# Windowed attention into a sine MLP: casting loads, denominators staged a unit ahead, Q copies on another engine, chunk tiles for x, one-bank MLP tiles

## The chip, the cores and the metric

The kernel runs on one core of one Trainium2 chip. The metric is the device time of one execution in microseconds (us), median of several; lower is better. A profile covers a slightly shorter span, from the first to the last instruction: 572.6 us for an execution that took 574.28 by the clock outside.

Engines are named as in the profile: PE is TensorE (PEld is its weight load), DVE is VectorE, ACT is ScalarE, POOL is GpSimd, SP is SyncE. In this kernel an instruction that is late also holds up what stands behind it on its engine: POOL's copies for batch 0, whose input DVE had ready at 82.9 us, ran only at 99.41, behind weight casts and load issues.

## The reference, cut to what matters

```python
# q, k, v: (8 batches, 8 heads, 576 tokens, 64);  8 global tokens
scores = (q @ k.T) / 8
mask   = (|i - j| <= 32) | is_global[i] | is_global[j]
attn   = softmax(where(mask, scores, -1e9)) @ v
x      = attn as (4608 tokens, 512)
h      = x @ w_in                      # 512 -> 2048
g      = h + sin(alpha * h)**2 / alpha
out    = g @ w_out                     # 2048 -> 512
```

## The kernel before

For each batch the kernel does attention in eight *units* (four pairs of heads, two halves of the token windows). The MLP works on nine chunks of 512 tokens. A steady *period* is: the first half of the MLP for one chunk ("MLP-in"), a short attention prologue, eight units of the next batch interleaved with the second half of the MLP ("MLP-out"), and an end that writes the eight global queries' columns. A unit, with cuts marked:

```python
def stage_V(b, hp, par, E, xTb, gn, gd):
    num = psA.tile([P, 2, CH], F32, name="num")      # one PSUM buffer of each name
    den = psA.tile([P, NU, QC], F32, name="den")
    ... # PE: den <- E by ones (2 matmuls); num <- E by V (6 matmuls)
    nc.scalar.activation(out=lnd[:], in_=den[:], func=AF.Ln)
    nc.scalar.activation(out=rec[:], in_=lnd[:], func=AF.Exp, scale=-1.0)   # 1/den
    for t in range(2):
        nc.vector.tensor_tensor(out=xTb..., in0=num..., in1=rec..., op=ALU.mult)  # products
    for t in range(2):
        nc.vector.tensor_reduce(out=gn..., in_=num[global columns], ...)
    nc.vector.tensor_reduce(out=gd..., in_=den[global columns], ...)        # last reader of den
```

MLP-in uses tiles of one or two PSUM banks in turn, and alpha has been folded into the weights on chip:

```python
CYC = (("h2", 1), ("num", 2), ("den", 1), ("Sp", 2))      # PSUM tiles, banks
h2 = w_inp @ x            # w_inp = w_in * alpha, cast to bf16 on DVE / POOL
Sb = sin(h2)              # ACT, up to two banks at once
S2 = Sb * Sb              # POOL, and DVE for a second bank
H2b = h2 + S2             # DVE;   w_outp = w_out / alpha on POOL
```

The Q transposes of the next batch sit inside MLP-in, and DVE copied them from PSUM (`qBD <- h2`). The eight global columns are written by POOL (`xTb[:, :, index] = xg`), and DVE then copies the batch into one tile for all of x.

The softmax here doesn't subtract the row's maximum and nothing guards it: scores larger than these inputs give would overflow.

Of the kernel before, what the change touches and what calls it, by code (L numbers as in the profile page):

```python
# [12 lines left out]
ALU = mybir.AluOpType  # L13
# [5 lines left out]
def kernel(  # L19
# [28 lines left out]
    NU = S // (2 * QB)  # L48
# [12 lines left out]
    rpool = ctx.enter_context(tc.tile_pool(name="rpool", bufs=2))  # L61
    xbp = ctx.enter_context(tc.tile_pool(name="xbp", bufs=2))
    gpool = ctx.enter_context(tc.tile_pool(name="gpool", bufs=2))

    psA = ctx.enter_context(
        tc.tile_pool(name="psA", bufs=1, space=bass.MemoryType.PSUM)
    )
# [5 lines left out]
    MASK = const.tile([P, 2, NU, QC], BF, name="MASK")  # L73
    w_inp = const.tile([P, CT, DFF], BF, name="w_inp")
    w_outp = const.tile([P, NT, DM], BF, name="w_outp")
    xT = const.tile([P, CT, NTOK], BF, name="xT")
    kTw = [const.tile([P, 2, NU, P], BF, name=f"kTw{i}") for i in range(NHP)]
    qBD = [const.tile([P, 2, NU, 2, QC], BF, name=f"qBD{i}") for i in range(NHP)]
# [3 lines left out]
    Kps = psA.tile([P, 2 * CH], BF, name="Kps")  # L82

    for i in range(2):
        nc.vector.memset(VW[i][0:32, 0, 0, :], 0.0)
        nc.vector.memset(VW[i][64:128, 1, NU - 1, :], 0.0)
        nc.vector.memset(VW[i][96:128, :, :, :], 0.0)


    def load_slots(b, split):  # L90
# [4 lines left out]
        slots = []  # L95
# [19 lines left out]
        for i in range(H if split else NTW):  # L115
            for src, dst in ((k, KS), (q, QS)):
                slots.append(partial(by_head if split else by_tile, src, dst, i))
# [19 lines left out]
    qk = {}  # L137
    for f in load_slots(0, True):
        f()


    make_identity(nc, identb[:])
    nc.vector.memset(ones0[:], 0.0)
# [6 lines left out]
    nc.vector.memset(Kps[:].bitcast(F32), 0.0)  # L150

    setup = tc.alloc_tile_pool(name="setup", bufs=1)
    gidx = setup.tile([1, NG], DT.int64, name="gidx")
    nc.sync.dma_start(out=gidx[:], in_=global_idx[None, :])
    gsc = const.tile([1, 2 * NG], DT.int32, name="gsc")
    nc.sync.dma_start(out=gsc[:].bitcast(DT.int64), in_=global_idx[None, :])

    gall = setup.tile([P, NG], DT.int64, name="gall")
    nc.sync.dma_start(
# [5 lines left out]
    nc.sync.dma_start(out=gcol[KB : KB + NG, :], in_=global_idx[:, None])  # L165
    gN = [setup.tile([NG * B, DM], F32, name=f"gN{i}") for i in range(3)]
    regs = {}

    def gather(i, src, eng, js):
        for j in js:  # L170
            if (eng, j) not in regs:
                regs[eng, j] = eng.value_load(
                    gsc[0:1, 2 * j : 2 * j + 1], min_val=0, max_val=S - 1
                )
            eng.dma_start(  # L175
                out=gN[i][j : NG * B : NG, :].rearrange("b (h d) -> b h d", d=D),
                in_=src[:, :, bass.ds(regs[eng, j], 1), :].rearrange("b h o d -> b h (o d)"),
            )

    gather(0, k, nc.sync, range(NG))  # L180
    gather(1, q, nc.scalar, range(NG))
    gather(2, v, nc.sync, range(0, NG, 2))
    gather(2, v, nc.scalar, range(1, NG, 2))
# [5 lines left out]
    nc.vector.tensor_copy(out=Gp[:], in_=gcol[:].bitcast(DT.int32)[:, 0:1])  # L189

# [14 lines left out]
    nc.gpsimd.affine_select(  # L205
        out=flag[:], in_=flag[:], compare_op=ALU.is_ge, fill=0.0,
        base=-KB, channel_multiplier=1, pattern=[[0, 1]],
    )
    nc.gpsimd.affine_select(
        out=flag[:], in_=flag[:], compare_op=ALU.is_ge, fill=0.0,  # L210
        base=KB + NG - 1, channel_multiplier=-1, pattern=[[0, 1]],
    )

    MB = setup.tile([P, NU, 2, QC], F32, name="MB")
    nc.gpsimd.memset(MB[:], 1.0)
    bandp = [[0, NU], [0, 2], [1, QB]]
    MBq = MB[:, :, :, 0:QB]

    nc.gpsimd.affine_select(
        out=MBq, in_=MBq, compare_op=ALU.is_ge, fill=0.0,  # L220
        base=0, channel_multiplier=1, pattern=[[0, NU], [0, 2], [-1, QB]],
    )

    nc.gpsimd.affine_select(
        out=MBq, in_=MBq, compare_op=ALU.is_ge, fill=0.0,
        base=2 * WIN, channel_multiplier=-1, pattern=bandp,
    )

    nc.gpsimd.affine_select(
        out=MBq, in_=MBq, compare_op=ALU.is_ge, fill=0.0,  # L230
        base=-WIN, channel_multiplier=1, pattern=[[2 * QB, NU], [QB, 2], [0, QB]],
    )
    nc.gpsimd.affine_select(
        out=MBq, in_=MBq, compare_op=ALU.is_ge, fill=0.0,
        base=S - 1 + WIN, channel_multiplier=-1, pattern=[[-2 * QB, NU], [-QB, 2], [0, QB]],
    )

    nc.gpsimd.affine_select(
        out=MBq, in_=MBq, compare_op=ALU.is_ge, fill=0.0,
        base=KB - 1, channel_multiplier=-1, pattern=[[0, NU], [0, 2], [0, QB]],  # L240
    )

    MBg = MB[:, :, :, QB:QC]
    nc.gpsimd.affine_select(
        out=MBg, in_=MBg, compare_op=ALU.is_ge, fill=0.0,
        base=-WIN, channel_multiplier=1, pattern=[[0, NU], [0, 2], [0, NG]],
    )
    nc.gpsimd.affine_select(
        out=MBg, in_=MBg, compare_op=ALU.is_ge, fill=0.0,
        base=WIN + QB - 1, channel_multiplier=-1, pattern=[[0, NU], [0, 2], [0, NG]],  # L250
    )
# [13 lines left out]
        out=MBq, in0=MBq, in1=DQ[:].rearrange("p (u a c) -> p u a c", a=2, c=QB),  # L265
        op=ALU.max,
    )
    nc.vector.tensor_copy(out=MASK[:].rearrange("p a u c -> p u a c"), in_=MB[:])

# [4 lines left out]
    nc.vector.tensor_copy(out=VgN[:], in_=gN[2][:])  # L274
    gps = psA.tile([P, 2, NHP, NG * B], BF, name="ops")
# [9 lines left out]
    )  # L285
    setup.release()
    pregs = [
# [3 lines left out]


    def globals_in(b, hp):
        nc.gpsimd.tensor_copy(
            out=kTw[hp][:, :, :, KB : KB + NG].rearrange("p a u g -> p (a u) g"),
            in_=GT[:, 0, hp, b, None, :].to_broadcast([P, 2 * NU, NG]),
        )
        for t in range(2):
            pr = slice(64 * t, 64 * t + 64)
            nc.gpsimd.tensor_copy(  # L300
                out=qBD[hp][pr, :, :, t, QB:QC].rearrange("p a u g -> p (a u) g"),
                in_=GT[pr, 1, hp, b, None, :].to_broadcast([64, 2 * NU, NG]),
            )

    def stage_T(b, hp):
        QS, KS = qk[b]
        for jt in range(NTW):
# [7 lines left out]
            out=kTw[hp][:, :, :, 0:KB],  # L315
            in_=bass.AP(
                tensor=base.tensor, offset=base.offset,
                ap=[list(base.ap[0]), [QB, 2], [2 * QB, NU], [1, KB]],
            ),
        )  # L320
        Qps = psA.tile([P, S], BF, name="h2")
# [6 lines left out]
        for t in range(2):  # L328
            pr = slice(64 * t, 64 * t + 64)
            nc.vector.tensor_copy(  # L330
                out=qBD[hp][pr, :, :, t, 0:QB].rearrange("p a u c -> p u a c"),
                in_=Qps[pr, :].rearrange("p (u a c) -> p u a c", a=2, c=QB),
            )
# [4 lines left out]
    def stage_Q(b, hp, par):  # L338
        Sp = psA.tile([P, 2, CH], F32, name="Sp")
        for u in range(NU):  # L340
            o = (u % HU) * 2 * QC
            nc.tensor.matmul(  # L342
                out=Sp[:, u // HU, o : o + 2 * QC],
                lhsT=kTw[hp][:, par, u, :],
                rhs=qBD[hp][:, par, u, :, :],
                start=True, stop=True, skip_group_check=True,
            )
# [5 lines left out]
            in1=MASK[:, par, :, None, :].to_broadcast([P, NU, 2, QC]),  # L353
# [4 lines left out]
    def stage_V(b, hp, par, E, xTb, gn, gd):  # L358
        W = VW[b % 2]
        num = psA.tile([P, 2, CH], F32, name="num")  # L360
        den = psA.tile([P, NU, QC], F32, name="den")
        for t, on in enumerate((ones0, ones1)):
# [5 lines left out]
            )  # L368
        for u in range(NU):
            o = (u % HU) * 2 * QC  # L370
            nc.tensor.matmul(
                out=num[:, u // HU, o : o + 2 * QC],
                lhsT=W[:, par, u, hp * P : (hp + 1) * P],
# [3 lines left out]
        lnd = rpool.tile([P, NU, QC], F32, name="lnd")  # L377
        nc.scalar.activation(out=lnd[:], in_=den[:], func=AF.Ln)  # L378
        rec = rpool.tile([P, NU, QC], F32, name="rec")
        nc.scalar.activation(out=rec[:], in_=lnd[:], func=AF.Exp, scale=-1.0)  # L380
        numv = num[:, :, 0:EW].rearrange("p a (u t c) -> p a u t c", t=2, c=QC)
        for t in range(2):
            pr = slice(64 * t, 64 * t + 64)
            xv = xTb[pr, hp, :].rearrange("p (a u r c) -> p a u r c", a=2, u=HU, r=2)
            nc.vector.tensor_tensor(  # L385
                out=xv[:, :, :, par, :],
                in0=numv[pr, :, :, t, 0:QB],
                in1=rec[pr, :, 0:QB].rearrange("p (a u) c -> p a u c", a=2),
                op=ALU.mult,
            )  # L390
        for t in range(2):
            pr = slice(64 * t, 64 * t + 64)
            nc.vector.tensor_reduce(  # L393
                out=gn[pr, par, hp, :],
                in_=numv[pr, :, :, t, QB:QC].rearrange("p a u c -> p c a u"),
                axis=mybir.AxisListType.XY, op=ALU.add,
            )
        nc.vector.tensor_reduce(  # L398
            out=gd[:, par, hp, :],
            in_=den[:, :, QB:QC].rearrange("p u c -> p c u"),  # L400
            axis=mybir.AxisListType.X, op=ALU.add,
# [15 lines left out]

    def attention(b):

        units = [(hp, par) for hp in range(NHP) for par in range(2)]  # L420
        Es = {}
        st = {}

# [241 lines left out]
```

## Time and profile before

575.36 us (573.01 to 576.26, three runs), span 572.6 us. The page of the profile gives each engine's busy time (first fence), and the view of stage windows gives it for one steady period (second fence). Its columns are: the stretch, its length, then for each engine busy us and instruction count, the clock granted to PE (1.00 is full), the DMA share and GB/s. The four rows are MLP-in, prologue, units and end; they sum to 58.2 us.

```profile
PE 362.7 (63%) x2396; PEld 186.8 (33%) x2440; DVE 331.5 (58%) x702; ACT 220.4 (38%) x343; POOL 307.9 (54%) x451
```

```profile
219.00:241.30 22.30, 17.17 (x86) 7.83 (x89) 12.65 (x19) 8.57 (x11) 12.90 (x21) 0.92 0.19 45
241.30:247.20 5.90, 4.13 (x42) 2.40 (x41) 3.97 (x7) 4.47 (x6) 5.32 (x6) 1.00 0.35 24
247.20:274.10 26.90, 18.03 (x152) 10.24 (x154) 18.88 (x56) 12.48 (x24) 11.41 (x16) 1.00 1.10 94
274.10:277.20 3.10, 1.26 (x6) 0.39 (x4) 0.91 (x2) 0.59 (x1) 1.62 (x8) 1.00 0.12 46
```

No engine is full in any stage. What the engines wait for stands in the view of waits (engine, line, result it wanted, what released it, us in total, times, longest):

```profile
PEld L363 <- DVE gd L398: 103.4, 56, 8.0
ACT lnd L378 <- PE den L363: 100.9, 59, 8.4
PE den L363 <- DVE gd L398: 82.4, 56, 7.7
DVE xTb L385 <- ACT rec L380: 57.3, 47, 1.8
PE h_854 L540 <- DVE xT L416: 22.8, 1, 22.8
```

The first four of these waits form a ring (`den` waits for `gd`, `lnd` for `den`, the products for `rec`), which the timeline shows in one unit (start, duration, engine, line, operation; in brackets how long the engine had stood idle and who released it):

```profile
264.00 0.32 PE L363 MATMUL den<-E,ones_77 128*128 128x336 bf16 x1 [1.24 <-DVE gd L398]
264.49 0.45 ACT L378 ACTIVATE lnd<-den 128x336 f32<-128x336 f32 x1 [1.56 <-PE den L363]
264.98 0.48 ACT L380 ACTIVATE rec<-lnd 128x336 f32<-128x336 f32 x1
265.49 0.92 DVE L385 TENSOR_TENSOR xTb<-num,rec 64x288 bf16<-64x288 f32 x2 [1.01 <-ACT rec L380]
266.45 0.42 DVE L393 TENSOR_REDUCE gn<-num 64x8 f32<-64x48 f32 x2
266.88 0.21 DVE L398 TENSOR_REDUCE gd<-den 128x8 f32<-128x48 f32 x1
267.15 0.32 PE L363 MATMUL den<-E,ones_77 128*128 128x336 bf16 x1 [1.54 <-DVE gd L398]
```

There is one `den` buffer. Its last reader is `gd`, a reduction of 0.21 us, which stands behind the products and `gn`; the products need `rec`; `rec` needs `lnd`; `lnd` needs `den`. So a unit takes at least the length of the ring, 3.15 us here.

The start is long too: the first MLP matmul runs at 102.32 us. The groups of instructions show the weight casts on it (count, busy us, mean ns):

```profile
L482 POOL TENSOR_SCALAR w_outp<-wtmp,recipT 128x512 bf16<-128x512 f32 x16 | 25.6, 1609 | 0.1
L466 DVE TENSOR_TENSOR w_inp<-wtmp,alphaB 128x2048 bf16<-128x2048 f32 x2 | 10.6, 5316 | 0.1
```

POOL gets to the eight column copies of batch 0 only at 99.41, behind the `w_outp` casts; DVE's last step before them had ended at 82.9. That is the wait of 22.8 us above.

### The profile page before, as it was taken

The numbers are of one execution on the slowest core, as the hardware profiler recorded it, in microseconds if no ns is written. First come the engines' busy times: TensorE is split into PE (matmuls) and PEld (weight loads), VectorE is DVE, ScalarE is ACT, GpSimd is POOL, SyncE is SP. The second block draws the span as 40 slices with busy tenths as digits, with TensorE's granted clock in tenths as the row PEclk, the third lists the DMA queues.
The fourth block names the chain that finished last, engine by engine and source line by source line (L and its number), as shares of the span: only waits on it lengthen the run. The fifth ranks groups of instructions, "written<-read, shape, count | busy, mean of one in ns | idle before, by whom it ended". The sixth has DMA issues, their size and how long they took to land.

```text
span 572.6 us, 7365 instructions
## 1 busy us (share of the span) xinstructions
PE 362.7 (63%) x2396; PEld 186.8 (33%) x2440; DVE 331.5 (58%) x702; ACT 220.4 (38%) x343; POOL 307.9 (54%) x451
## 2 busy tenths in 40 slices
PE   0124220776586768666866587767676767678996
PEld 0123210334333433243334333433343334333443
DVE  7448940458547854685568536663776476647430
ACT  0013210425444544354435442644364426444431
POOL 9743999459146904690459136832792361037430
PEclk9999999979999999899989988999999989999999
DMA  9977955409630943095309630993099300000011
GB/s 90 113 111 292 279 69 36 64 0 115 53 89 0 125 45 88 1 120 48 89 1 114 54 89 2 81 86 89 0 94 76 88 1 18 20 37 1 37 38 74
DMA packets 132202, 40.48 MB, mean 71 GB/s; under 512 B 123204, under 2 KB 123972, under 8 KB 131524
## 3 DMA queue, kind: packets, MB, share of 16 engines
q0 software_dynamic: 118208, 14.82, 40.8%
q1 hardware_dynamic: 13092, 24.99, 14.1%
q8 instruction: 19, 0.31, 0.2%
q10 hardware_dynamic: 864, 0.20, 0.2%
q14 instruction: 19, 0.16, 0.1%
HBM read 39.47 MB, written 9.44 MB: 85 GB/s over the span
## 4 chain that ended last, share of the span: by engine, by line
issue 28%; POOL 24%; PE 20%; DVE 8%; ACT 7%; DMA 6%; ACTq 3%; SPq 1%; POOLq 0%; DVEq 0%
PE num L540 7%; ACT Sb L547 5%; POOL w_outp L482 4%; PE ops L576 4%; POOL QS L103 3%; POOL KS L103 3%; DVE H2b L525 3%; PE Sp L540 3%; DMA QS<-in_q_dram 2%; POOL VW_92 L110 2%; POOL xTb L413 2%; ACTq L175 2%; DMA wtmp<-in_moe_w_in_dram 2%; POOL w_inp L466 2%; ACT L547 1%
## 5 line engine op out<-in xcount | busy, mean ns | idle before, releaser
L576 PE MATMUL ops<-w_outp,H2b 128*128 128x512 bf16 x412 | 103.1, 379 | 1.7 <-ACT osb L583 0.7
L540 PEld LDWEIGHTS <-w_inp 128*128 128x128 bf16 x576 | 58.3, 104 | 138.2 <-issue 49.8
L385 DVE TENSOR_TENSOR xTb<-num,rec 64x288 bf16<-64x288 f32 x128 | 58.2, 455 | 58.4 <-ACT rec L380 57.3
L413 POOL COPY xTb<-xg 128x4 bf16 x64 | 13.0, 203 | 127.6 <-DVE xg L411 124.1
L363 PE MATMUL den<-E,ones_77 128*128 128x336 bf16 x64 | 21.3, 333 | 89.8 <-DVE gd L398 82.4
L378 ACT ACTIVATE lnd<-den 128x336 f32<-128x336 f32 x64 | 28.9, 452 | 111.8 <-PE den L363 100.9
L576 PEld LDWEIGHTS <-H2b 128*128 128x128 bf16 x576 | 52.2, 98 | 49.0 <-issue 1.0
L349 ACT ACTIVATE E<-Sp 128x672 bf16<-128x672 f32 x64 | 46.6, 729 | 48.0 <-PE Sp L342 47.7
L540 PE MATMUL num<-xT,w_inp 128*128 128x512 bf16 x204 | 58.7, 426 | 4.2 <-DVE H2b L525 3.3
L547 ACT ACTIVATE Sb<-num 128x1024 bf16<-128x1024 f32 x27 | 27.7, 1024 | 37.1 <-PE num L540 34.9
L363 PEld LDWEIGHTS <-ones_77 128*128 128x128 bf16 x64 | 6.2, 97 | 104.2 <-DVE gd L398 103.4
L351 DVE TENSOR_TENSOR E<-E,MASK 128x672 bf16<-128x672 bf16 x64 | 32.6, 512 | 9.3 <-ACT E L349 8.1
L540 PE MATMUL Sp<-xT,w_inp 128*128 128x512 bf16 x140 | 33.6, 379 | 0.2
L103 POOL DMA_DIRECT2D KS<-in_k_dram x42 | 33.0, 786 | 0.0
L103 POOL DMA_DIRECT2D QS<-in_q_dram x42 | 32.4, 772 | 0.0
L380 ACT ACTIVATE rec<-lnd 128x336 f32<-128x336 f32 x64 | 31.0, 484 | 2.0
L547 ACT ACTIVATE Sb<-Sp 128x1024 bf16<-128x1024 f32 x18 | 18.4, 1025 | 30.6 <-PE Sp L540 30.6
L308 PE MATMUL Kps<-identb,KS 96*128 96x96 bf16 x192 | 14.4, 214 | 23.9 <-POOL identb masks.py:199 19.6
L540 PE MATMUL den<-xT,w_inp 128*128 128x512 bf16 x108 | 28.4, 387 | 0.0
L393 DVE TENSOR_REDUCE gn<-num 64x8 f32<-64x48 f32 x128 | 26.2, 205 | 2.6
L583 ACT COPY osb<-ops 128x512 f32<-128x512 f32 x27 | 15.8, 585 | 30.1 <-PE ops L576 30.1
L547 ACT ACT_TABLE_LOAD x8 | 10.3, 1283 | 41.6 <-PE h_854 L540 24.3
(480 smaller groups left out, 758.8 us busy)
## 6 DMA issues: line engine op xcount, KB each, us to landing
out_dram<-osb SPq DMA_DIRECT2D x36, 256.0 KB
wtmp<-in_moe_w_in_dram SPq DMA_DIRECT2D x4, 1024.0 KB
wtmp<-in_moe_w_out_dram SPq DMA_DIRECT2D x4, 1024.0 KB
KS<-in_k_dram POOLq DMA_DIRECT2D x42, 96.0 KB, 4.0
QS<-in_q_dram POOLq DMA_DIRECT2D x42, 96.0 KB, 4.3
VW_91<-in_v_dram POOLq DMA_DIRECT2D x20, 112.0 KB, 4.2
VW_92<-in_v_dram POOLq DMA_DIRECT2D x20, 112.0 KB, 4.2
VW_91<-VW_91 SPq DMA_DIRECT2D x4, 384.0 KB
```

Source lines behind the costliest of these rows:

```text
L103: nc.gpsimd.dma_start(out=dst[:, t, :, :], in_=src[b, :, t * TW : (t + 1) * TW, :].rearrange("h p d -> p h d"),)
L349: nc.scalar.activation(out=E[:], in_=Sp[:, :, 0:EW], func=AF.Exp, scale=scale)
L351: nc.vector.tensor_tensor(out=Ev, in0=Ev, in1=MASK[:, par, :, None, :].to_broadcast([P, NU, 2, QC]), op=ALU.mult,)
L363: nc.tensor.matmul(out=den[:].rearrange("p u c -> p (u c)"), lhsT=on[:], rhs=E[:].rearrange("p a (u t c) -> p (a u) t c", t=2, c=QC)[:, :, ...
L378: nc.scalar.activation(out=lnd[:], in_=den[:], func=AF.Ln)
L380: nc.scalar.activation(out=rec[:], in_=lnd[:], func=AF.Exp, scale=-1.0)
L385: nc.vector.tensor_tensor(out=xv[:, :, :, par, :], in0=numv[pr, :, :, t, 0:QB], in1=rec[pr, :, 0:QB].rearrange("p (a u) c -> p a u c", a=2 ...
L393: nc.vector.tensor_reduce(out=gn[pr, par, hp, :], in_=numv[pr, :, :, t, QB:QC].rearrange("p a u c -> p c a u"), axis=mybir.AxisListType.XY ...
L413: nc.gpsimd.tensor_copy(out=xTb[:, :, bass.ds(pregs[j], 1)], in_=xg[:, :, j : j + 1])
L540: nc.tensor.matmul(out=h2[:, k_, :], lhsT=w_inp[:, ci, (nt + k_) * P : (nt + k_ + 1) * P], rhs=xT[:, ci, t0 : t0 + CH], start=(ci == 0), s ...
L547: nc.scalar.activation(out=Sb[:, 0:n, :], in_=h2[:], func=AF.Sin)
L576: nc.tensor.matmul(out=ops[:], lhsT=H2b[:, nt, ts * P : (ts + 1) * P], rhs=w_outp[:, nt, :], start=(nt == 0), stop=(nt == NT - 1),)
```

## The change

The intent: take the weight casts off the engines by letting the load cast; compute the denominators a unit ahead, so that Ln and Exp are done when the products want them; relieve DVE of the Q copies; keep x in small tiles of one chunk; and use six one-bank tiles in MLP-in. Its core, with cuts marked:

```diff
-            wtmp = wst.tile([P, DFF], F32, name="wtmp")
-            nc.sync.dma_start(out=wtmp[:], in_=moe_w_in[c * P : (c + 1) * P, :])
-            ... eng.tensor_tensor(out=w_inp[:, c, :], in0=wtmp[:], in1=alphaB[:], op=ALU.mult)
+            nc.gpsimd.dma_start(out=w_in[:, c, :], in_=moe_w_in[c * P : (c + 1) * P, :])   # casts
 ... # w_out likewise, issued in the first MLP-in stage
-            nc.vector.tensor_copy(out=qBD[hp]..., in_=Qps...)
+            nc.scalar.copy(out=qBD[hp]..., in_=Qps...)
 ...
+    def stage_D(psA, hp, hf, E, gd):
+        den = psA.tile([P, NU, QC], F32, name="den")
+        ... # den matmuls, Ln, Exp
+        nc.vector.tensor_reduce(out=gd[:, hf, hp, :], in_=den[global columns], ...)
+        return rec
-    def stage_V(b, hp, par, E, xTb, gn, gd):
-        ... # den, num, Ln, Exp, products, gn twice, gd
+    def stage_V(psA, b, hp, hf, E, rec, xTb, gn):
+        ... # num, products, gn once
 ...
                 if j + 2 < n:
                     Es[j + 2] = stage_Q(psA, b, *units[j + 2])
+                if 0 <= j + 1 < n:
+                    recs[j + 1] = stage_D(psA, *units[j + 1], Es[j + 1], gd)
 ...
-        nc.vector.tensor_copy(out=xT[:, :, b * S : (b + 1) * S], in_=xTb[:])
+        ... # copies into tiles xC[c] of 512 tokens, three buffers
 ...
-                h2 = psA.tile([P, n, CH], F32, name=tag)             # n = 1 or 2 banks
-                nc.scalar.activation(out=Sb[:, 0:n, :], in_=h2[:], func=AF.Sin)
-                ... # add: H2b = h2 + S2
+                h2 = psB.tile([P, CH], F32, name="hb")               # 6 buffers of one bank
+                nc.scalar.activation(out=Sb[:], in_=h2[:], func=AF.Sin, scale=alphaT[:, nt:nt+1])
+                ... # add: H2b = S2 * recipT + h2, one scalar_tensor_tensor
```

`stage_D` has the `den` matmuls, Ln, Exp and `gd`, and `stage_V` the `num` matmuls, the products and `gn`: in DVE's program, `gd` now comes before the products.

## The prediction

> **What bounds the kernel now.** Chains; no engine is full (page, part 1: PE 63%, DVE 58%, POOL 54%, ACT 38% of 572.6 us). From timeline and stage windows:
>
> 1. Start, 102.3 us before the first MLP matmul. The mask is ready at 37.5, but VectorE sits 5.8 us on the reciprocal of the late alpha load; the first masked multiply starts at 43.5. Its w_in casts (5.8, 4.9) stop units. VectorE's last step ends at 82.9, but the GpSimd column copies start at 99.4, behind w_out casts (16 of 1.6 us) and load issues; PE waits 22.8 (waits view).
> 2. Seven periods of about 58 us (distance of first Sins). Windows of one: MLP-in 22.3, attention prologue 5.9, eight units 26.9, end 3.1; PE busy 40.6 of 58.2.
>    - Units: 3.15 to 3.4 us each, a loop den -> Ln 0.45 -> Exp 0.48 -> two products 0.92 -> gn 0.42 -> gd 0.21 -> den (waits view, 82.4).
>    - MLP-in: PE needs 13.8 us. Two-bank Sin (1.02), GpSimd square (1.28) and add (1.23) in series, and Q copies on VectorE, make it 22.
> 3. Last 63 us: MLP-in of chunk 7 (17), 27.8 of matmuls that fill PE, then 14.
>
> **What the change does.**
>
> - Start: weight casts (GpSimd 9.5+25.6 us, VectorE 10.6) vanish; the load casts. alpha and index columns load early, so the mask multiply should begin near 30, units take 2.6, eight 21, end 4: first MLP matmul near 57, saving 45. The weights' 8 MB join the k/q/v loads in one queue; the next batch's k/q/v or w_out may arrive late: up to 5.
> - Unit: Ln and Exp leave the loop. VectorE is left: mask 0.51, gd 0.21, products 0.92, one gn of 96 elements (estimate 0.27 from 0.205 for 48), K copy 0.85 in a quarter of units: 2.1. PE, with interleaved matmuls, 2.2 to 2.4. So 2.3 instead of 3.3: saves 7 to 8 a period. ScalarE gains Q copies [...]: not limiting.
> - MLP-in: one-bank tiles, six buffers. Per four: PE 3.46, POOL three squares 3.4, VectorE four adds of 0.7 and a square, 3.2, ScalarE four Sins. [...] GpSimd's copies of globals, 3.4 in a lump, cost about 2. Sum 17.5 instead of 22.
> - Prologue and end 7.5 instead of 9.
> - Period: 17.5 + 18.5 + 7.5 plus slips = about 46.5. Tail about 61.5.
>
> **Sum.** 57 + 51 (first period) + 6 x 46.5 + 61.5 + 2.7 (time outside the span) = about 451; with slips I predict **456 us**, 8 in 10 between 436 and 488. Chances: faster by over 2% 0.97, within 2% 0.02, slower 0.01.
>
> **What would show it.** First MLP matmul at 52 to 65 us; no GpSimd TENSOR_SCALAR on w_out; "den on gd" gone from the top of the waits; first Sins 44 to 50 apart; DVE near 85% in units; PE near 78% busy; [...] MLP-in 17 to 19.
>
> **What would make it wrong.** Casting loads much slower than the plain 1 MB loads, so that the first two periods wait on DMA; GpSimd squares (1.04 alone, 1.28 beside a VectorE square) bounding MLP-in; units bound by latency between engines rather than 2.3 (ScalarE's order: E, Ln, Exp, Q copies)[...].

The sum came to about 451 us, and to 456 with slips; every term of it stands. The Sin's price had been put below PE's share of MLP-in, so the 17.5 us of that stage do not change.

## The result, and the profile after

443.7 us (440.0 to 444.18, four runs) against 574.85 us for the kernel before in the same rounds. The ratio is 0.7706, with a 95% interval of 0.7659 to 0.7753. Here and below a ratio is the mean time of one kernel's runs over that of the other's of the same rounds, so it is not quite the ratio of the medians quoted. All outputs were correct, in this and in every run below.

The same views of the kernel after: the page's busy times, then the windows of one steady period, which now sum to 44.7 us.

```profile
PE 346.8 (78%) x2396; PEld 183.1 (41%) x2440; DVE 298.1 (67%) x628; ACT 269.3 (61%) x453; POOL 275.1 (62%) x447
```

```profile
201.30:218.20 16.90, 15.06 (x85) 6.98 (x85) 11.61 (x17) 14.03 (x21) 13.69 (x23) 1.00 0.23 60
218.20:222.60 4.40, 1.77 (x16) 1.06 (x17) 4.40 (x8) 2.75 (x4) 4.40 (x6) 1.00 0.38 24
222.60:242.60 20.00, 19.08 (x172) 11.41 (x175) 15.66 (x45) 14.32 (x29) 11.72 (x16) 1.00 1.46 114
242.60:246.00 3.40, 2.67 (x13) 1.17 (x12) 1.02 (x4) 0.58 (x1) 1.61 (x8) 1.00 0.21 77
```

The waits: the ring's lines on `gd` are gone, the wait of the products on `rec` is no longer among the long ones, and what is left in the units is PE's weight load behind `gn`, which frees the single `num` buffer.

```profile
ACT Sb L472 <- PE hb L465: 35.8, 57, 7.8
PEld L375 <- DVE gn L392: 24.7, 48, 1.8
ACT lnd L359 <- PE den L352: 23.0, 16, 4.4
PE den L352 <- DVE E L342: 16.4, 8, 4.4
```

A late unit in the timeline, from `gn` to `gn`, is 1.76 us, and `gd` is out of the way before the products start:

```profile
236.07 0.26 DVE L392 TENSOR_REDUCE gn<-num 128x16 f32<-128x96 f32 x1
236.36 0.51 DVE L342 TENSOR_TENSOR E<-E,MASK 128x672 bf16<-128x672 bf16 x1
236.40 0.46 PE L375 MATMUL num<-E,VW_104 128*128 128x112 bf16 x6
236.79 0.20 DVE L362 TENSOR_REDUCE gd<-den 128x8 f32<-128x48 f32 x1
236.91 0.91 DVE L384 TENSOR_TENSOR xTb<-num,rec 64x288 bf16<-64x288 f32 x2
237.83 0.26 DVE L392 TENSOR_REDUCE gn<-num 128x16 f32<-128x96 f32 x1
```

The group of Sins with alpha as their scale, from the page's costliest groups:

```profile
L472 ACT ACTIVATE Sb<-hb,alphaT 128x512 bf16<-128x512 f32 x144 | 94.5, 687 | 42.8 <-PE hb L465 35.8
```

And the two weight loads, from the page's DMA issues (count, KB written by each, median us from issue to landing):

```profile
w_in<-in_moe_w_in_dram POOLq DMA_DIRECT2D x4, 512.0 KB, 7.9
w_out<-in_moe_w_out_dram POOLq DMA_DIRECT2D x4, 512.0 KB, 11.4
```

Where the time went can be read from the start of each chunk's first MLP matmul in the timeline:

| stretch (us) | before | after | predicted | saved |
|---|---|---|---|---|
| start, to the first MLP matmul | 102.3 | 58.5 | 57 | 43.8 |
| first period | 61.0 | 53.0 | 51 | 8.0 |
| six steady periods, each | 57.7 | 44.8 | 46.5 | 12.9 (six: 77.2) |
| tail, from the last chunk's first matmul that way | 63.2 | 61.6 | 61.5 | 1.6 |
| span | 572.6 | 442.0 | about 448 | 130.6 |

Each stretch agrees with the prediction to 2 us; the six steady periods together came 10 us shorter than predicted (268.9 against 279). That does not yet say that the *reasons* were right, so the parts were taken apart.

### The profile page after: what moved, and what is told of

It is laid out like the page before. It is cut to its first block, busy times and chain, and to the rows that moved or that the text cites. A ratio compares the mean times of both kernels' runs of the same rounds, so it can differ in the third digit from the quotient of the medians. Undisturbed runs are those within 1.5% of the kernel's fastest.

```text
span 442.0 us, 7238 instructions
## 1 busy us (share of the span) xinstructions
PE 346.8 (78%) x2396; PEld 183.1 (41%) x2440; DVE 298.1 (67%) x628; ACT 269.3 (61%) x453; POOL 275.1 (62%) x447
## 4 chain that ended last, share of the span: by engine, by line
POOL 33%; issue 27%; PE 16%; DVE 13%; DMA 5%; ACT 3%; POOLq 2%; ACTq 0%
DVE H2b L455 7%; PE ops L499 6%; PE hb L465 6%; DMA QS<-in_q_dram 4%; POOL QS L105 3%; POOL VW_104 L112 3%; POOL KS L105 3%; POOL VW_105 L112 3%; POOL xTb L411 3%; PE hb L499 2%; ACT L472 1%; POOL QS L100 1%; ACT Sb L472 1%; POOL KS L100 1%; POOLq L277 1%
## 5 line engine op out<-in xcount | busy, mean ns | idle before, releaser
L465 PE MATMUL hb<-xC,w_in 128*128 128x512 bf16 x559 | 134.1, 383 | 19.0 <-DVE xC L418 10.0
L472 ACT ACTIVATE Sb<-hb,alphaT 128x512 bf16<-128x512 f32 x144 | 94.5, 687 | 42.8 <-PE hb L465 35.8
L499 PE MATMUL ops<-w_out,H2b 128*128 128x512 bf16 x412 | 105.8, 384 | 2.0 <-ACT osb L506 0.7
L465 PEld LDWEIGHTS <-w_in 128*128 128x128 bf16 x576 | 56.3, 98 | 89.0 <-issue 28.7
L411 POOL COPY xTb<-xg 128x4 bf16 x64 | 12.9, 201 | 85.3 <-DVE xg L409 81.9
L359 ACT ACTIVATE lnd<-den 128x288 f32<-128x288 f32 x64 | 26.2, 409 | 23.0 <-PE den L352 23.0
L352 PE MATMUL den<-E,ones_89 128*128 128x336 bf16 x64 | 20.3, 317 | 16.9 <-DVE E L342 16.4
L361 ACT ACTIVATE rec<-lnd 128x288 f32<-128x288 f32 x64 | 28.4, 443 | 2.0
L499 PE MATMUL qp<-w_out,H2b 128*128 128x512 bf16 x105 | 27.7, 379 | 0.4
L112 POOL DMA_DIRECT2D VW_105<-in_v_dram x28 | 21.4, 785 | 0.0
L333 PE MATMUL Sp<-qBD_100,kTw_96 128*128 128x112 bf16 x96 | 8.1, 227 | 16.9 <-DVE H2b L455 10.5
L375 PE MATMUL num<-E,VW_104 128*128 128x112 bf16 x192 | 15.0, 215 | 8.0 <-DVE gn L392 7.2
L112 POOL DMA_DIRECT2D VW_104<-in_v_dram x28 | 21.2, 768 | 0.0
L352 PE MATMUL den<-E,ones_90 128*128 128x336 bf16 x64 | 20.4, 319 | 0.0
## 6 DMA issues: line engine op xcount, KB each, us to landing
w_out<-in_moe_w_out_dram POOLq DMA_DIRECT2D x4, 512.0 KB, 11.4
```

The costliest lines, as they stand in the source:

```text
L112: nc.gpsimd.dma_start(out=W[p0 : p0 + n, par, u, :].rearrange("p (h d) -> p h d", d=D), in_=v[b, :, key0 : key0 + n, :].rearrange("h p d - ...
L352: nc.tensor.matmul(out=den[:].rearrange("p u c -> p (u c)"), lhsT=on[:], rhs=E[:].rearrange("p a (u t c) -> p (a u) t c", t=2, c=QC)[:, :, ...
L359: nc.scalar.activation(out=lnd[:], in_=den[:, :, 0:QB], func=AF.Ln)
L465: nc.tensor.matmul(out=h2[:], lhsT=w_in[:, ci, nt * P : (nt + 1) * P], rhs=xC[c][:, ci, :], start=(ci == 0), stop=(ci == CT - 1),)
L472: nc.scalar.activation(out=Sb[:], in_=h2[:], func=AF.Sin, scale=alphaT[:, nt : nt + 1])
L499: nc.tensor.matmul(out=ops[:], lhsT=H2b[:, nt, ts * P : (ts + 1) * P], rhs=w_out[:, nt, :], start=(nt == 0), stop=(nt == NT - 1),)
```

## The experiments

"The changed kernel" is the kernel after; each edit is against it unless said otherwise. Every run is quoted with the ratio to the kernel before of its own rounds, whose medians were 574.72 to 575.62 us. Differences in us are of medians, to the changed kernel's 443.7; the runs are of different rounds, so a difference of a few us is to be read with their spread in mind.

### 1. Denominators back in their own unit

```diff
-                if 0 <= j + 1 < n:
-                    recs[j + 1] = stage_D(psA, *units[j + 1], Es[j + 1], gd)
 ...
                 if j >= 0:
+                    recs[j] = stage_D(psA, *units[j], Es[j], gd)
                     stage_V(psA, b, *units[j], Es.pop(j), recs.pop(j), xTb, gn)
```

> The changed kernel with the denominator stage back in its own unit, but with the small sum gd still straight after Ln and Exp, ahead of the two products. Theory 1 (the prediction): being a unit ahead is what takes Ln and Exp out of the loop; undone, a unit needs about 0.5 (den) + 0.41 + 0.44 + 0.92 + 0.26 plus hops, 2.9 to 3.2 us in place of 2.5, so 470 to 485 us. Theory 2: the loop was closed by the place of gd behind the products, which frees the one den bank late; with gd early PE can send the next den while the products run, so this run loses little: 444 to 455 us, units 2.5 to 2.7.

Measured: 445.2 us (444.06 to 445.81), ratio 0.7743 (0.7717 to 0.777). That is 1.5 us more than the changed kernel, and the intervals overlap. So the headline of this part, "a unit ahead", is worth next to nothing by itself. `den` here still has `gd` early, so the next unit's `den` matmuls, Ln and Exp run under this unit's products anyway.

### 2. The same, and gd back behind the products

```diff
                 if j >= 0:
+                    recs[j], dn = stage_D(psA, *units[j], Es[j], gd)   # without gd
                     stage_V(psA, b, *units[j], Es.pop(j), recs.pop(j), xTb, gn)
+                    stage_gd(*units[j], dn, gd)                        # gd last, as before
```

> As the run before, and gd moved back behind the products and gn, as the old kernel had it. Both theories: the old loop den, Ln, Exp, products, gn, gd is closed again, a unit 2.9 to 3.2 us: 470 to 485 us. If it is equal to the run before, the place of gd doesn't matter (theory 1); if it is 15 us or more slower, it does (theory 2).

Measured: 481.29 us (480.37 to 481.96), ratio 0.8371. Moving one reduction of 0.2 us behind the products costs 36.1 us against the run before it (481.29 − 445.2). The ring is back in its view of waits, the same links as in the kernel before; the two waits on `gd` are shorter than there (73.8 and 53.0 us against 103.4 and 82.4), the wait on `rec` is longer (66.2 against 57.3):

```profile
PEld L352 <- DVE gd L394: 73.8, 56, 2.0
DVE xTb L379 <- ACT rec L361: 66.2, 63, 1.8
PE den L352 <- DVE gd L394: 53.0, 56, 1.8
```

From the Sin table loads in the timeline, the steady period is 49.3 us instead of 44.8.

### 3. Only gd moved, in the kernel before

If the place of `gd` is the cause, the old kernel must gain from it with nothing else changed.

```diff
         nc.scalar.activation(out=rec[:], in_=lnd[:], func=AF.Exp, scale=-1.0)
+        nc.vector.tensor_reduce(out=gd[:, par, hp, :], in_=den[global columns], ...)
         ... # products, gn
-        nc.vector.tensor_reduce(out=gd[:, par, hp, :], in_=den[global columns], ...)
```

> The OLD kernel with one statement moved: the sum gd stands straight after the reciprocal, ahead of the two products; the denominator stage stays in its unit. Theory 2 (the place of gd closed the loop): units fall from 3.15 to 3.4 us to about 2.6, some 5 us in each of 7 periods: 535 to 548 us, and the wait of den on gd, 82.4 us, falls below 20. Theory 1 (Ln and Exp must be a unit ahead) or a VectorE bound: 565 to 576.

Measured: 537.56 us (535.57 to 537.95), ratio 0.9348 (0.9331 to 0.9365). One statement moved by a few lines gives 37.6 us (575.17 − 537.56), a period of 52.4 us instead of 57.7. PE's wait of `den` on `gd` falls from 82.4 to 14.2 us, as expected. A faster clock is not the reason: the granted clock was lower than before, 0.926 against 0.975. So the gain was there in the old structure, and needs neither the staging ahead nor another buffer. Experiments 1 to 3 settle this point.

### 4. Q copies back on VectorE

```diff
-            nc.scalar.copy(
+            nc.vector.tensor_copy(
                 out=qBD[hp][pr, :, t, 0:QB],
```

> The changed kernel with the Q copies on VectorE again (two of about 0.46 us per head pair, eight in a period, 3.7 us of VectorE more in about 45, ScalarE 5 us less). Theory (PE bounds the units, 19.1 busy of 20.0 in the window of one, and VectorE has 4 us to spare): 446 to 455 us. Rival (VectorE still bounds units and MLP-in): all 3.7 us come back in each of 7 periods, 465 to 470.

Measured: 457.49 us (456.8 to 458.07), ratio 0.7957. The move is worth 13.8 us, more than the theory's range and less than the rival's. The steady period is 46.5 us, 1.6 more than in the changed kernel, and 1.1 of this lies in MLP-in (17.34 against 16.28 us between its two table loads); the rest is in the start and the first period, whose second Sin table load comes 3.3 us later (115.79 against 112.54).

### 5. Plain weight loads and engine casts

The kernel loads fp32 weights by plain loads into the two buffers of `H2b`, which are free at the start, and casts them with a multiply by one: DVE and POOL for `w_in`, POOL for `w_out`. It is not the old code exactly: the operand of ones is broadcast, and its `w_in` casts take 2.28 us on DVE where the old ones took 5.32. The figure is therefore rather too small for what the casts cost before.

```diff
-   nc.gpsimd.dma_start(out=w_in[:, c, :], in_=moe_w_in[c * P : (c + 1) * P, :])
+   nc.sync.dma_start(out=wtmp, in_=moe_w_in[c * P : (c + 1) * P, :])
+   eng.tensor_tensor(out=w_in[:, c, :], in0=wtmp, in1=ones, op=ALU.mult)     # DVE / POOL
 ... # w_out: plain load, then 16 POOL tensor_scalar
```

> The changed kernel with plain fp32 loads of the weights on SyncE's queue and the same multiplies as in the old kernel (by one), two on VectorE, two and sixteen on GpSimd, in the places of the old kernel; alpha stays in the Sin scale and in the add. Theory: only the start changes: first MLP matmul at 82 to 95 in place of 58.5 us, since two multiplies of 5.3 us stop VectorE and GpSimd gets 35 us of work before its column copies; in the second half of the start the loads leave the casting queue, the first period is perhaps 2 shorter. 465 to 480 us. Rival (the start waits on loads or on PE): under 455.

Measured: 469.13 us (467.04 to 469.59), ratio 0.8146: 25.4 us for the casts. All of it arises in the start. The first MLP matmul runs at 88.90 instead of 58.47, again behind a wait of 20.8 us for x, because the column copies on POOL stand behind the casts:

```profile
88.90 11.41 PE L467 MATMUL hb<-xC,w_in 128*128 128x512 bf16 x38 [20.80 <-DVE xC L420]
```

Its second Sin table load is at 137.47, against 112.54 (24.9 later), and after that its periods are those of the changed kernel, 44.9 us against 44.8.

### 6. One tile for x

```diff
+    xT = const.tile([P, CT, NTOK], BF, name="xT")
 ...
-        ... # copies into xC[c]
+        nc.vector.tensor_copy(out=xT[:, :, b * S : (b + 1) * S], in_=xTb[:])
```

To make room for it in SBUF, `lnd` got one buffer instead of two (ACT ran the Exp straight behind its Ln in that run too: 0.41 us from 37.95, then 0.44 us from 38.40) and the MLP's pools were opened after the setup pool was released.

> The changed kernel with one x tile for all tokens and one copy of 2304 elements (0.76 us) a batch in place of two into chunk tiles (0.83 us). For room, the pools of H2b and its scratch are opened after the setup, and lnd has one buffer (ScalarE takes Ln and Exp in order, so that should cost nothing). Theory: worth nothing in time, 441 to 447 us; the chunk tiles buy SBUF. Rival (the wait of the first MLP matmul on the copy gets shorter by the split): 447 to 452.

Measured: 449.62 us, but 444.7 to 449.88, ratio 0.7789 (0.7742 to 0.7835). The median is 5.9 us up, in the rival's range, and the fastest run 1.0 us, in the theory's; the interval overlaps the changed kernel's. Part of it is the clock: in the profiled run two of six steady periods were at a granted clock of 0.96 and took 46.58 us, where the changed kernel has one. A period at full clock takes 45.02 us against 44.40 to 44.73. The chunk tiles are worth between nothing and 6 us, and the two helper edits are inside that figure. What the chunk tiles surely give is room: three tiles of 4 KB per partition instead of one of 36 KB.

### 7. Two-bank tiles in MLP-in

```diff
-                h2 = psB.tile([P, CH], F32, name="hb")
+                if nt % 2 == 0: pair.append(psB.tile([P, 2, CH], F32, name="hb"))
+                h2 = pair[-1][:, nt % 2, :]
 ... # matmuls, Sin, square and add as before
-        with phase_pool("psB", 6) as psB:
+        with phase_pool("psB", 3) as psB:
```

> The changed kernel with MLP-in tiles of two banks, three buffers, so the same six banks; Sin, square and add stay one bank each. Only the size of what is given back changes, and a Q transpose takes two banks for its one. Theory: buffers come free up to 0.9 us later, 1 to 3 us in each of 8 MLP-in stages: 450 to 465 us. Rival (GpSimd's squares bound MLP-in, so buffers are idle anyway): 442 to 447.

Measured: 528.21 us (526.89 to 529.47), ratio 0.9182, 84.5 us more. This is too much for the old arrangement, and the waits show why: PE waits on Sin 64 times, for the 72 pairs of tiles.

```profile
PE hb L468 <- ACT Sb L475: 64.8, 64, 2.1
```

In program order the second bank's matmuls stand behind the first bank's Sin, and PE waited for that Sin on the *other* bank (198.59, after the Sin of 197.85 to 198.54). In this kernel, then, the wait goes by the tile and not by the bank. This run measures my edit.

### 8. Four one-bank tiles instead of six

```diff
-        with phase_pool("psB", 6) as psB:
+        with phase_pool("psB", 4) as psB:
```

> The changed kernel with four banks in place of six for MLP-in. A tile is held for matmuls 0.9, Sin 0.7, square 1.0, add 0.7 and the two tiles of lag of the add, about 4.5 us; four banks then give a tile every 1.1 us in place of 0.9. Theory (depth of banks matters): 3 to 5 us in each of 8 stages, 465 to 482 us. Rival (GpSimd squares bound the stage): 442 to 450.

Measured: 476.12 us (475.44 to 477.1), ratio 0.8274. Two buffers fewer cost 32.4 us; the period is 49.3 us and MLP-in about 21 us. The rival expected no loss. So with three engines (ACT, POOL or DVE, DVE) between a tile's last matmul and its release, four tiles are not enough to keep PE going. The run doesn't say what bounds the stage with six: there the timeline has POOL busy with squares and global copies without a gap of 0.1 us from 204.01 to 219.89, while PE's last MLP-in matmul ended at 217.42. No run took squares off POOL, so POOL as a second bound at six tiles stays open.

### 9. Two-bank tiles again, both matmul groups before both Sins

```diff
 ... # tiles of two banks; mm holds the matmuls, post the Sin, square and add
+            def slot(nt=nt, mm=mm, post=post):
+                mm()
+                if nt % 2:
+                    post(nt - 1)      # Sin, square, add of the first bank
+                    post(nt)          # and of the second
 ... # three buffers
```

> Two-bank tiles again, but mended: the run u_two_bank showed 64.8 us of PE waiting for Sin, 64 times, because the matmuls into the second bank came behind the Sin of the first bank of the same tile in program order, and waits are kept by tile. Here both matmul groups stand ahead of both Sins, as the old kernel had it. What is left is the later start of the first Sin (0.86 us) and the later return of two banks at once: three buffers held for about 6 us give a pair every 2.0 us in place of 1.73: 2 to 4 us in each of 8 MLP-in stages, 455 to 475 us, and the wait of PE on Sin gone. If it stays at 500 or more, the tile size itself costs the 84 us and not the order.

Measured: 492.36 us (490.6 to 494.39), ratio 0.8553, granted clock 0.938. That is 48.7 us more than six one-bank tiles with the same six banks, and above the range expected. The wait on Sin is gone, as intended, and PE waits for the adds instead (24.2 us in 17 waits). Once a stage it also waits for the Q copies (15.0 us in 8 waits), because a Q transpose takes a whole two-bank tile of three. So granularity counts and not only the number of banks. The windows of the six steady MLP-in stages show the clock's part: two were at a clock of 1.00 and took 20.64 us, four at 0.86 to 0.92 and took 21.71 to 23.84, and the changed kernel's take 16.28. So 4.4 of the 5.6 us that a stage lost on average are lost at full clock. How they divide between the release two banks at a time and the Q transpose that takes two banks stays open.

### 10. PE work moved from the units into the prologue

In the changed kernel PE is busy for 19.08 of the 20.0 us of the units, and for only 1.77 of 4.4 us in the prologue. If PE bounds the units, moving MLP-out matmuls into the prologue must help.

```diff
 ... # in attention: early runs between the second score stage and the first den
+                early = [fill.pop(2)] if fill else []
+                parts, last = attention(p, psA, early)      # one slot before the first den
+                if fill:
+                    parts[0] = partial(chain, parts[0], fill.pop(0), fill.pop(0))
 ... # the first three parts run without filling, the other slots are spread over the rest
```

> Not an undoing: the changed kernel with the second product's first three slots of four matmuls put into the attention prologue (two after the first score stage, one between the second score stage and the first denominators), where PE was busy 1.77 of 4.4 us; the other nine slots spread over the units, where PE was busy 19.1 of 20.0. Theory (PE bounds the units): each period shorter by 1 to 2 us, 430 to 437 us. Rival (VectorE bounds the units): no gain, 441 to 446.

Measured: 449.57 us (448.37 to 450.47), ratio 0.782 (0.7785 to 0.7856): 5.9 us slower. The windows of prologue and units:

```profile
221.30:225.70 4.40, 3.34 (x24) 1.79 (x25) 4.40 (x8) 2.76 (x4) 4.40 (x6) 1.00 0.39 25
225.70:246.00 20.30, 17.08 (x164) 10.15 (x164) 15.09 (x42) 14.42 (x29) 11.76 (x16) 1.00 1.43 113
```

PE does 2.0 us less work in the units, and they take 20.3 us instead of 20.0. So PE's work does not bound them although PE was busy for 95% of the time. (The prologue stays at 4.40 us; DVE is busy in all of it here and in the changed kernel.) PE's waits on `gn` rise from 9.2 to 25.8 us: PE's slack turned into waiting for the `num` buffer. A busy share close to one was a symptom of good interleaving and no limit.

### 11 and 12. The index column early, and the column copies on VectorE

The mask waits for a column of global indices. In the changed kernel its load is issued at 16.26, behind the gathers on ACT's queue, and the mask is ready at 35.4. Experiment 11 is experiment 10 with that load first and with DVE writing the global columns in place of POOL.

```diff
+    gcol = const.tile([P, 1], DT.int64, name="gcol")
 ... # memset
+    nc.scalar.dma_start(out=gcol[KB : KB + NG, :], in_=global_idx[:, None])
 ... # the same lines cut further down; the edits of experiment 10
-        nc.gpsimd.value_load(gsc[0:1, 2 * j : 2 * j + 1], ...)
+        nc.vector.value_load(gsc[0:1, 2 * j : 2 * j + 1], ...)
-            nc.gpsimd.tensor_copy(out=xTb[:, :, bass.ds(pregs[j], 1)], in_=xg[:, :, j : j + 1])
+            nc.vector.tensor_copy(out=xTb[:, :, bass.ds(pregs[j], 1)], in_=xg[:, :, j : j + 1])
```

> i_fill and two more: the index column's memset and load are first on their queues, so the mask should be there at about 30 in place of 35.4 us; and VectorE, not GpSimd, writes the eight columns of global queries at the end of a batch (2.05 us and two hops on GpSimd). Theory: start 4 to 5 us shorter, end of a batch 1 to 2 us shorter less what PE fills anyway, so 6 to 12 us below i_fill, 420 to 430 us. If VectorE's register loads land in the middle of its busy start, the start gains less.

Measured: 452.61 us (451.46 to 453.12), ratio 0.7865, slower than experiment 10. The mask was ready at 28.0, but DVE then loaded eight registers before it could go on, and the gain was lost:

```profile
34.74 0.86 DVE L305 COPY kTw<-Kps 128x1344 bf16<-128x1344 bf16 x1 [6.38 <-issue]
```

The steady period, though, was 0.4 us shorter than in experiment 10 (45.1 against 45.5). So experiment 12 drops the moved PE work, keeps the early index column, leaves batch 0's columns to POOL, and places DVE's register loads after batch 0, where DVE had idled.

```diff
+        eng, rg = (nc.gpsimd, pregs) if b == 0 else (nc.vector, vregs)
-            nc.gpsimd.tensor_copy(out=xTb[:, :, bass.ds(pregs[j], 1)], ...)
+            eng.tensor_copy(out=xTb[:, :, bass.ds(rg[j], 1)], ...)
+        if b == 0:
+            ... # the eight nc.vector.value_load, after batch 0's chunk copy
```

> The changed kernel with the index column's memset and load first on their queues (so the mask should be there at about 28 to 30 us instead of 35.4) and, from the second batch on, VectorE instead of GpSimd writing the eight global-query columns; VectorE's eight register loads stand after batch 0's chunk copy, where it idled 4.25 us. Theory, that the start waits for the mask: the start is 4 to 5 us shorter, and the end of each later batch about 0.45 us shorter (as the run with all three edits showed), so 434 to 439 us. Rival, that the start is bounded by the global columns' copies and the first Sp tile whatever the mask does: 440 to 446 us. If the register loads (6.4 us for eight in the earlier run) outlast the idle time, the first MLP-in stage is later by 2 us or so and the gain is smaller by that.

Measured, in five rounds: 441.38 us (440.26 to 441.49), ratio 0.7672 (0.7654 to 0.769). It is 2.3 us below the changed kernel's median, but the intervals overlap, so it is not shown to be faster. The steady periods are shorter by 0.38 us, as expected: from the second to the eighth Sin table load it takes 266.7 us, and the changed kernel 269.0. The start was not shortened; the first MLP matmul runs at 60.33 and not at 58.47. The timeline says why:

```profile
27.75 0.16 DVE L206 TENSOR_REDUCE flag<-EQ 128x1 f32<-128x8 f32 x1 [6.71 <-POOL EQ L201]
28.44 0.41 DVE L260 CAST gB<-gN 64x512 bf16<-64x512 f32 x1
30.54 0.74 DVE L249 TENSOR_TENSOR MASK<-MB,DQ 128x576 bf16<-128x576 f32 x1
31.21 0.41 DVE L269 COPY GT<-ops 128x512 bf16<-128x512 bf16 x1
36.94 0.51 DVE L343 TENSOR_TENSOR E<-E,MASK 128x672 bf16<-128x672 bf16 x1 [2.98 <-ACT E L341]
```

The mask was ready at 31.3, four us earlier. But with the index column there early, the setup's order on DVE changed: the mask's steps now stood ahead of the casts of the gathered global rows, and DVE waited 6.71 us on a POOL step first. The casts ran at 28.4 instead of 22.3, the global copies and the first scores followed, and the first masked multiply began at 36.94 instead of 35.52. Two chains of nearly equal length meet in front of the first unit, and shortening one by lengthening the other gains nothing.

### What the parts add up to

Undone one at a time, the parts cost: `gd` and its stage 37.6 us (481.29 − 443.7), six one-bank tiles 32.4 us (to four tiles) to 48.7 us (to two-bank pairs), weights 25.4, Q copies 13.8, x tiles 0 to 6. Together that is 109 to 132 us of the 131 us gained. The sum is near the gain, but that the parts add up is shown only for `gd`, which is worth about the same in both kernels; no run undid two of the other parts together. Not taken apart at all are the single `gn`, Ln and Exp over 288 columns instead of 336, and the order of the setup.

## Why the prediction was right or wrong, point by point

**The number was right**: 456 predicted, 436 to 488 as the range, 443.7 measured; 97% was given to "faster by over 2%".

**The start: right in sum, wrong in one step.** "First MLP matmul near 57" came at 58.5. The weight casts vanished, as predicted, and experiment 5 shows that they alone were worth about 25 us. But "the mask multiply should begin near 30" failed: it began at 35.5. I had seen that the index column's load was moved and took it to be early, while in the trace it is issued at 16.26, behind the gathers on the same queue, and POOL's steps on the flags then stand behind copies and load issues. Faster units in the first attention made up for it, so that the sum came within 1.5 us is in part luck. Experiment 12 shows that the mask was not alone in holding the start: with the mask ready four us earlier the start was no shorter.

**Late data from the casting loads: did not happen.** I reserved up to 5 us for late data. The kernel issues all eight casting loads from GpSimd, and they landed in 7.9 us (`w_in`) and 11.4 us (`w_out`, medians of four each). Whether plain loads of the weights land sooner is not shown: the page of the kernel before gives no time to landing for its own. No wait of PE on them is in the view of waits. POOL itself stood idle 7.7 us in all, behind them, before later load issues.

**The units: right in mechanism, wrong in what brings it about.** "Ln and Exp leave the loop" is what happened, and "saves 7 to 8 a period" came to 6.9 (26.9 to 20.0). But the change was described as denominators computed a unit ahead, and the prediction took that over without asking which of its two effects counts. I listed `gd` as 0.21 us of DVE work; I even wrote it down as the last link of the ring ("gd 0.21 -> den") and did not see that its *place* is what closes the ring. Experiment 1 takes the staging away and loses 1.5 us; experiment 2 takes the early `gd` away as well and loses 36.1 more; experiment 3 gives it to the old kernel and wins 37.6. The units' gain is the early release of the single `den` buffer.

**"PE, with interleaved matmuls, 2.2 to 2.4", so units of 2.3: off by a little, and PE is not the bound.** The eight units take 20.0 us, 2.5 each; those with a K copy take longer and the late ones 1.8. PE is busy 95% of it, which looks like the predicted bound, and experiment 10 shows that it is not: with 2.0 us less of PE work the units take as long. In the late units shown above the chain `num` -> products -> `gn` -> `num` runs with hardly a gap and takes all of the 1.76 us; that this chain and DVE's order of work set the pace of all eight is argued, since no run gave `num` a second buffer. DVE's own busy share is 78% (15.66 of 20.0) against the "near 85%" predicted.

**MLP-in: "17.5 instead of 22", measured 16.9 instead of 22.3.** The traces show 687 ns for a Sin with alpha as its scale (kernel after) and 595 ns for one without it (kernel before) on the same 512 columns, 92 more. The rival named in the prediction, that GpSimd's squares bound the stage, is not excluded: experiment 8 shows that four tiles are too few, and with six POOL has no idle gap from its first square on.

One term was missing from the prediction altogether: PE's clock. In the window of the kernel before PE is busy for 17.17 us in MLP-in, and after for 15.06, with the same MLP-in matmuls. Once in each MLP-in stage of the old kernel PE waited 2.50 us for the Q copies, which stood behind an add and a K copy on DVE, and in five of the seven stages the matmuls after that ran slowly (the clock over the whole stage was 0.82 to 0.92 in these five and 1.00 in the other two). The timeline of the kernel before shows the wait:

```profile
236.24 1.85 PE L540 MATMUL h_2136<-xT,w_inp 128*128 128x512 bf16 x4 [2.50 <-DVE qBD_88 L330]
```

The view of windows of the same kernel shows the clock just after it, third value from the end, at 0.54:

```profile
237.00:240.00 3.00, 3.00 (x9) 1.16 (x8) 0.44 (x1) 0.60 (x1) 1.04 (x1) 0.54 0.00 0
```

Those four matmuls took 1.85 us, and four undisturbed ones of the same stage 1.03 to 1.04. What makes the clock fall is not shown: all seven stages have the same wait of 2.50 us, and two of them kept the full clock. These two separate the clock from the tiles. Here are one of the two, one of the slowed ones, and one of the kernel after, each from the Sin table load to the next table load:

```profile
164.42:184.50 20.08, 15.37 (x91) 7.45 (x92) 12.75 (x20) 9.56 (x12) 13.32 (x22) 1.00 0.13 29
220.54:242.31 21.77, 17.06 (x91) 7.89 (x92) 12.76 (x20) 9.56 (x13) 13.33 (x22) 0.92 0.12 27
157.27:173.55 16.28, 14.47 (x83) 6.70 (x82) 11.63 (x17) 14.03 (x21) 13.72 (x23) 1.00 0.23 51
```

The slowed stage is 1.7 us longer, and PE's busy time is longer by the same 1.7 us. Between the two stages at full clock 3.8 us are gained. The period chosen for the windows above has a slowed stage in the kernel before, which flatters MLP-in's gain by that much. All six steady stages of the kernel after are at 1.00. Putting the Q copies back on DVE (experiment 4) did not bring the slow clock back there (1.00 in its six steady stages too); no run shows why.

**The first period: 51 predicted, 53.0 measured.** In the first chunk every second square is on DVE, and some of them took much longer than the 0.41 to 0.43 us of those with no GpSimd square beside them: 2.21, 1.54 and 2.41 us. The one of 2.41 us runs from 80.01 to 82.42, and two GpSimd squares fill 80.09 to 82.13; the other two ended about a us after the GpSimd square beside them. What lengthened them is not shown. At the end of that chunk, at 83.2, PE had waited 4.01 us for an add and it ran at a clock of 0.50 from 85 to 88 us. The chunk's first matmuls were slow as well, at a clock of 0.51 from 58.47 to 63.40. No experiment separated these; the extra 2 us are only argued.

**Prologue and end: 7.5 predicted, 7.8 measured. Tail: 61.5 predicted, 61.6 measured**; PE is busy for 55.9 us of it before and after, and the change hardly touches it.

## What to carry to other kernels

When a single PSUM buffer is on a ring of engines, look for its last reader before planning anything larger: moving one 0.2 us reduction ahead of the products was worth 36 to 38 us in both kernels, where computing the whole stage a unit ahead added 1.5, which is within the spread. A busy share of 95% does not make an engine the limit; take work away from it and see whether the stage gets shorter. In this matmul stage, whose results pass through several engines, six one-bank tiles beat three of two banks by 48.7 us, clock and Q transposes included. Look at the granted clock of the same stage in every period before a gain is put down to the code: here it moved a stage by 1.7 us.
